# Windowed attention and feed-forward on one core: a handicap for VectorE in the planner's choice of engine, an own buffer for transposed blocks, no stores of A21, five late groups instead of six

## Chip, core and metric

The kernel runs on one NeuronCore of a Trainium2 chip. A core has TensorE (PE; its weight loads are shown as PEld), VectorE (DVE), ScalarE (ACT), GpSimd (POOL) and SyncE (SP), which here issues all DMAs from one queue. The metric is the device time of one execution in microseconds, the median of several; lower is better. All five engines run their own instruction streams in order and meet at semaphores.

## The reference

```
scores = q @ k^T / 8 + ALiBi bias, masked to 0 <= i - j < 128    # 8 batches, 8 heads, 576 tokens, 64 wide
attn   = softmax(scores);  x = attn @ v                           # -> x: 4608 tokens x 512
h      = x @ w_in                                                 # 512 x 2048
g      = h if h >= 1, 0 if h <= -1, else (h + 1)^2 / 4
out    = g @ w_out                                                # 2048 x 512
```

All of it is float32. The two weight matrices arrive as 64-bit numbers and are made float32 in the kernel.

## The kernel before, in words

**Work and stages.** The 4608 tokens are cut into nine chunks of 512. For each chunk there is attention (8 heads; head m is counted through all chunks, m = 0 to 71) and then a "sweep" of the feed-forward over eight groups g of two feature blocks. While chunk c is swept, the attention of chunk c + 1 is mixed in, so TensorE alternates between the two. Matrix products that need float32 are done in the rounded format FP32R with operands split into a rounded part and the rest (`rounded`, L362, and a subtraction), three products for one.

**First layer.** In chunk 0 each group multiplies four plain weight blocks A11, A12, A21, A22 with the token blocks B11 to B22. From chunk 1 on it uses a scheme of seven products (`PRODUCTS`, L30), whose weight operands are A11, A12, A22 and the four sums S1 to S4 of blocks (A21 enters only the sums). `build` (L506) makes a split operand in SBUF and stores it to a scratch buffer `d_<g>_<name>` in DRAM (shown as d_A and d_S); `fetch` (L519) brings it back in the later chunks (w_A, w_S). The ring of these operands has ten buffers, and `operands_upto` (L976) asks for them ten ahead.

**Early and late groups.** For the groups with g < 8 - LATE the sums are built during chunk 0 and fetched in chunk 1; there they pass the two buffers "o" that second-layer weights and outputs use too. For the last LATE groups (`late`, L981) the float32 weights are stored in chunk 0 (`spill`, d_w), loaded again in chunk 1 (`unspill`, L483) and the sums are built then, straight into the ring. LATE is 6 (L326).

**Attention.** Scores (L671 to L674), a masked copy (L680), a subtraction with the row minimum (L683) and the exponential (L687), the normalisation of z by the row sums (L698 on VectorE or four instructions L696 on ScalarE), a transposition of z, a split into lu0 and lu1 with masks on GpSimd (L705 on), and the product with v (L820), whose result is added into xn. Up to head 27 the transposition is TensorE's (p, L760); from head 28 (`TURN`) `turn_blocks` (L719) does it with VectorE's block transposition (L729) and two DMAs through DRAM (d_turn), in one buffer named turned.

**Second layer and activation.** `nonlinear` (L890): m = ReLU(h + 1) (L894 on VectorE or L895 on ScalarE), m squared (L897, ScalarE), h from it (L899), and the split into gh and gl. `layer2` multiplies gh and gl with the second-layer weights wo (L915 to L917, bank acc).

**What sets the order.** Every step is given to a planner (`Plan`) with its possible engines, each with a cost in microseconds, in the order of preference: `rounded` prefers ScalarE, the ReLU on SBUF prefers VectorE, the normalisation prefers VectorE. `forward` (L168) walks through time: whenever an engine e comes free it takes the ready step with the earliest due time. If e is not the step's first choice it asks first whether that choice would be done sooner (L222 to L226, the lines that the change touches):

```
queue = max(0.0, free[first] - t) + sum(...)          # what waits on the first choice
if queue + n.alts[first][0] < busy + 0.1:
    held_back = True
    continue
```

Twelve rounds with corrected due times are planned, the one that ends first is kept, and the program is written in its order: each engine runs its rows as they stand, whatever happens on the chip. So a change in one rule plans all engines anew.

**Shared buffers.** 17 buffers "w" (`NW`, L418) hold raw weights, the second-layer weights, the reloaded weights of the late groups (w32) and, once all of these have a place, the buffer turned (L724 to L726).

Of the kernel before, what the change touches and what calls it, by code (L numbers as in the profile page):

```python
# [9 lines left out]
F32 = mybir.dt.float32  # L10
# [19 lines left out]
PRODUCTS = (("A11", "B11"), ("A12", "B21"), ("S2", "T2"), ("S3", "T3"), ("S1", "T1"), ("S4", "B22"), ("A22", "T4"))  # L30
# [26 lines left out]
class Plan:  # L57


    CROSS, SAME, BACKLOG, STRETCH, SWAP, ROUNDS = 0.09, 0.04, 4.0, 2.0, 8.0, 12  # L60

    def __init__(self):
        self.nodes, self.slots, self.turn, self.common = [], {}, {}, {}
# [104 lines left out]
    def forward(self, engines, bandwidth):  # L168
        free = {e: 0.0 for e in engines}
# [11 lines left out]
        def room(n, t):  # L181
            b = n.need
            if b is None:
                return True
            free = sum(x <= t + 1e-9 for x, _ in slots[b.tag])
            return free > 0 and b.fits(free)

        def wake(e, t):
            nonlocal tick
            tick += 1  # L190
            heapq.heappush(events, (max(t, free[e]), tick, e))

        def enter(n):
            for e in n.alts:
                r = 0.0
                for d in n.deps:
                    r = max(r, d.end + (self.SAME if d.eng == e else self.CROSS))
                avail[e].append((n, r))
                wake(e, r)
# [6 lines left out]
        while events:  # L206
            t, _, e = heapq.heappop(events)
            if free[e] > t + 1e-9 or not avail[e]:
                continue
            if e == "SP" and pipe > t + self.BACKLOG:  # L210
                wake(e, pipe - self.BACKLOG)
                continue
            cands = [(n.late, n.index, n, r) for n, r in avail[e] if r <= t + 1e-9 and room(n, t)]
            if not cands:
                continue
            cands.sort(key=lambda x: x[:2])
            pick, held_back = None, False
            for late, _, n, r in cands:
                busy = n.alts[e][0]
                first = next(iter(n.alts))  # L220
                if first != e:
                    queue = max(0.0, free[first] - t) + sum(m.alts[first][0] for m, q in avail[first]  # L222
                                                            if m is not n and q <= t + 0.2 and m.late < n.late)
                    if queue + n.alts[first][0] < busy + 0.1:
                        held_back = True
                        continue  # L226
                worse = [(m, q) for m, q in avail[e] if q > t + 1e-9 and q < t + busy - 0.05 and m.late < late - 0.2
                         and m.late + slip < t + busy]
                if e in ("PE", "SP") or not worse:
                    pick = n  # L230
                    break
                soon = min(q for _, q in worse)
                if soon - t > 0.5 * busy:
                    pick = n
                    break
            if pick is None:
                soon = [q for _, q in avail[e] if q > t + 1e-9]
                wake(e, min(soon + [t + 0.2] if held_back else soon))
                continue
            if e == "DVE" and pick.alts[e][3] and lock["POOL"] > t + 0.15:  # L240
                for late, _, n, r in cands:
                    if not n.alts[e][3] and late < pick.late + self.SWAP and next(iter(n.alts)) == e:
                        pick = n
                        break
            n = pick
            busy, lat, _, port = n.alts[e]
            if port and e in lock:
                other = "POOL" if e == "DVE" else "DVE"
                held = max(0.0, lock[other] - t)
                busy, lat = busy + held, lat + held  # L250
                lock[e] = t + busy
            n.eng, n.start = e, t
            if e == "SP":
                pipe = max(pipe, t + lat) + port / bandwidth
                n.end = pipe + 0.2
            else:
                n.end = t + lat
            if n.need is not None:
                at = min((x for x in slots[n.need.tag] if x[0] <= t + 1e-9))
                slots[n.need.tag].remove(at)  # L260
                n.need.slot = at[1]
            for b in n.uses:
                if b.tag:
                    b.left, b.last = b.left - 1, max(b.last, n.end)
                    if not b.left:
                        slots[b.tag].append((b.last + self.CROSS, b.slot))
                        for x in engines:
                            wake(x, b.last + self.CROSS)
                    elif n.need is b:
                        for x in engines:  # L270
                            wake(x, t)
            free[e] = t + busy
            if e == "PE":
                slip = max(0.0, t - n.nominal)
            order.append(n)
            done += 1
            for x in n.alts:
                avail[x] = [a for a in avail[x] if a[0] is not n]
            wake(e, free[e])
            for s in n.next:  # L280
                waits[s] -= 1
                if waits[s] == 0:
                    enter(s)
# [13 lines left out]
def windowed_attention_then_ffn(  # L297
# [9 lines left out]
    nc = tc.nc  # L307
# [4 lines left out]
    P = 128  # L312
# [10 lines left out]
    NEG = -1.0e30  # L323
    LIGHT = 8
    FIRST = 1
    LATE = 6  # L326
    LO = D + 2
    TURN = 28
    assert set(SIZES) == {4}
# [1 line left out]
    plan = Plan()  # L331
    pools = {}
# [6 lines left out]
    def buf(pool, tag, n, shape, dtype, name):  # L339
        return plan.buf(pools[pool], tag, n, shape, dtype, name)  # L340
# [6 lines left out]
    def dve(n, f, port=False):  # L347
        return {"DVE": (n * 0.00104 + 0.068, n * 0.00104 + 0.155, f, port)}
# [13 lines left out]
    def rounded(n, out, src):  # L362

        alts = act(n, lambda: S.copy(out(), src()))  # L364
        alts.update(dve_fast(n, lambda: V.tensor_copy(out(), src())))
        return alts
# [7 lines left out]
    def dma(nbytes, f):  # L374
        return {"SP": (0.4, 2.8, f, nbytes)}
# [38 lines left out]
    w_of, wo_of, raw, fo, raws, kept = {}, {}, {}, {}, [], []  # L414
# [3 lines left out]
    NW = 2 * NFC + 1 - NFC  # L418
# [56 lines left out]
    scratch, sums_w, spilled, unspilled = {}, {}, {}, []  # L475
# [30 lines left out]
    def build(g, name):  # L506
        b, key, f = operand(g, name)
        if name in PLAIN or g >= NG - LATE:
            t = buf("ring", "r", 10, [P, 2, 2, P], F32R, f"b_{g}_{name}")
        else:  # L510
            t = buf("fp", "o", 2, [P, 2, 2, P], F32R, f"b_{g}_{name}")
        plan.op(rounded(2 * P, lambda: t.t[:, 0], f), [(b, key)], [(t, 0)])
        plan.op(dve(2 * P, lambda: V.tensor_tensor(t.t[:, 1], f(), t.t[:, 0].bitcast(F32), ALU.subtract), True),
                [(b, key), (t, 0)], [(t, 1)])
        d = scratch[g, name] = plan.buf(dr, f"d_{g}_{name}", 1, [P, 4 * P], F32, f"d_{g}_{name}")
        plan.op(dma(P * 2048, lambda: DMA.dma_start(d.t, t.t.bitcast(F32).rearrange("p s c f -> p (s c f)"))), [t], [d])
        return t
# [199 lines left out]
    turned = []  # L717

    def turn_blocks(m, z):  # L719


        if not turned:
            turned.append(plan.shared(pools["wp"], "w", NW, [P, 2, 4 * P], F32, "turned", lambda free: (
                all(x.slot is not None for _, x in kept) and all(x.slot is not None for x in unspilled))))  # L724
        t = turned[0]
        d = plan.buf(dr, "d_turn", 2, [P, 4 * P], F32, f"d_turn_{m}")  # L726

        def block():
            V.transpose(t.t[:, 0].rearrange("p (b i j) -> p b i j", b=4, i=4), z.t.rearrange("p i (s b) -> p b i s", b=4))  # L729

        plan.op(dve(4 * P, block, True), [z], [(t, 0)])
        plan.op(dma(P * 2048, lambda: DMA.dma_start(d.t, t.t[:, 0])), [(t, 0)], [d])
        plan.op(dma(P * 2048, lambda: DMA.dma_start(
            t.t[:, 1].rearrange("p (a e) -> p a e", a=4), d.t.rearrange("(a s) (b e) -> (s b) a e", a=4, b=4))), [d], [(t, 1)])
        return (t, 1), lambda: t.t[:, 1].rearrange("p (a i j) -> p i a j", a=4, i=4)
# [240 lines left out]
    def operands_upto(n):  # L976
        while asked[0] < min(n, len(todo_w)):
            c, g, x = todo_w[asked[0]]
            if c == 0 and x == "A11":
                weights_upto(4 * g + 2)  # L980
            late = g >= NG - LATE  # L981
            if late and c == 1 and x == "A11":
# [103 lines left out]
    for c in range(NCHUNK):  # L1086
        steps = sweep_steps(c)
        n = len(steps)
# [46 lines left out]
```

## Time and profile before

| | |
|---|---|
| median of 3 runs | 964.62 us (964.22 to 964.88) |
| profiled execution | 964.71 us, of which 963.0 us from the first to the last instruction (the span) |
| busy: PE / PEld / DVE / ACT / POOL | 951.1 / 863.4 / 869.9 / 661.4 / 218.5 us |
| moved by DMA | 227.40 MB, mean 236 GB/s |

How to read it: the profile is one execution. Every instruction belongs to a source line (L12 is line 12 of the kernel), an operation and tiles (out<-in, buffer numbers left out). Busy time of TensorE includes pipelining, so a busy TensorE can still be held up for a few tenths; its empty time is the part that can be read directly. "Idle" is followed by what ended it. The chain of waits is followed back from the last instruction. Times in the windows count from the start of the span.

### The profile page before, as it was taken

To read this page: it belongs to the slowest core of one execution; us is meant where nothing else is said; L and a number is where in the kernel's file an instruction comes from. 1 tells how busy PE (TensorE), PEld (TensorE's weight loads), DVE (VectorE), ACT (ScalarE), POOL (GpSimd) and SP (SyncE) were. 2 spreads that over 40 slices of the span, in tenths; PEclk is the share of its full clock that TensorE was granted. 3 is DMA by queue.
4 is the path that set the end of the run, shared out by engine and by line. 5 is a ranking of instruction groups with operands and counts; after the bars stand their busy time and mean duration, and the time that the engine had idled before them with its cause. 6 is when DMAs were issued, how large, how long until landed. Compare 5 with 4: busy or idle time off the path is not lost.

```text
span 963.0 us, 19573 instructions
## 1 busy us (share of the span) xinstructions
PE 951.1 (99%) x6320; PEld 863.4 (90%) x6320; DVE 869.9 (90%) x2183; ACT 661.4 (69%) x1657; POOL 218.5 (23%) x274
## 2 busy tenths in 40 slices
PE   8999999999999999999999999999999999999998
PEld 7889998999889998999899989899899999989987
DVE  6999999999999999999999999999999999984453
ACT  7998777877887677665876577667766777553322
POOL 2311111222331222322232212312232222210000
PEclk9999999999999999999999999999999999999999
DMA  9678886676867876887788869787888778766651
GB/s 345 235 244 276 300 269 204 229 220 222 246 204 255 253 243 211 284 259 245 223 278 254 255 212 279 244 255 223 257 276 251 218 233 272 225 174 201 174 152 44
DMA packets 133237, 227.40 MB, mean 236 GB/s; under 512 B 13712, under 2 KB 36240, under 8 KB 133136
## 3 DMA queue, kind: packets, MB, share of 16 engines
q1 hardware_dynamic: 133136, 226.15, 74.7%
q8 instruction: 51, 0.84, 0.3%
q14 instruction: 50, 0.41, 0.1%
HBM read 185.20 MB, written 40.89 MB: 235 GB/s over the span
## 4 chain that ended last, share of the span: by engine, by line
PE 83%; DVE 7%; ACT 6%; DMA 3%; issue 1%; POOL 0%; SPq 0%; ACTq 0%; DVEq 0%; POOLq 0%
PE hA L883 17%; PE hB L883 13%; PE acc L916 12%; PE acc L915 12%; PE acc L917 12%; PE x L820 6%; PE h L883 3%; PE s L673 2%; PE s L674 2%; ACT z L687 2%; PE s L671 1%; ACT raw L451 1%; DMA raw<-in_moe_w_out_dram 1%; PE p L760 1%; ACT raw L461 1%
## 5 line engine op out<-in xcount | busy, mean ns | idle before, releaser
L915 PE MATMUL acc<-wo,gh 128*128 128x512 f32 x576 | 228.0, 396 | 0.1
L916 PE MATMUL acc<-wo,gh 128*128 128x512 f32 x576 | 227.3, 395 | 0.0
L917 PE MATMUL acc<-wo,gl 128*128 128x512 f32 x576 | 225.7, 392 | 0.2
L708 POOL TENSOR_SCALAR_AFFINE_SELECT lu<-lu 128x512 fp32r<-128x512 f32 x112 | 100.6, 898 | 516.5 <-ACT lu L364 179.6
L1025 ACT COPY s<-hA 128x256 f32<-128x256 f32 x192 | 70.8, 369 | 98.7 <-PE hA L883 93.5
L687 ACT ACTIVATE z<-z,nmax 128x128 f32<-128x128 f32 x288 | 113.3, 395 | 26.9 <-DVE nmax L683 25.6
L917 PEld LDWEIGHTS acc<-wo,gl 128*128 128x128 f32 x576 | 108.2, 188 | 25.6 <-DVE gl L903 1.4
L915 PEld LDWEIGHTS acc<-wo,gh 128*128 128x128 f32 x576 | 108.9, 189 | 9.8 <-DVE o L923 0.3
L916 PEld LDWEIGHTS acc<-wo,gh 128*128 128x128 f32 x576 | 109.1, 189 | 8.8
L897 ACT ACTIVATE m<-m 128x512 f32<-128x512 f32 x144 | 90.6, 630 | 28.2 <-DVE m L894 26.3
L899 DVE SCALAR_TENSOR_TENSOR h<-h,m 128x512 f32<-128x512 f32 x128 | 95.0, 743 | 12.3 <-ACT m L897 11.7
L883 PEld LDWEIGHTS hA<-x_T,w_S 128*128 128x128 f32 x696 | 95.4, 190 | 8.7 <-ACT s L1025 3.1
L883 PE MATMUL hA<-x_T,w_S 128*128 128x256 f32 x696 | 102.2, 283 | 1.0 <-ACT s L1025 1.0
L1020 DVE TENSOR_TENSOR h<-hB,s 128x256 f32<-128x256 f32 x192 | 79.7, 415 | 24.8 <-PE hB L883 20.6
L903 DVE TENSOR_TENSOR gl<-h,gh 128x512 fp32r<-128x512 f32 x128 | 91.2, 713 | 1.9 <-ACT gh L364 0.7
L711 POOL TENSOR_SCALAR_AFFINE_SELECT lu<-lu 128x512 fp32r<-128x512 f32 x112 | 92.9, 851 | 0.0
L683 DVE CUSTOM_DVE_ANT_0 z<-s,rel 128x128 f32<-128x128 f32 x288 | 70.8, 282 | 0.5
L680 DVE COPY_PREDICATED s<-older,s 128x256 f32<-128x256 uint32 x144 | 59.8, 420 | 9.4 <-PE s L671 5.1
L364 ACT CAST gh<-h 128x512 fp32r<-128x512 f32 x75 | 46.5, 620 | 24.9 <-DVE h L899 24.0
L820 PE MATMUL x<-lu,vs 128*128 128x256 f32 (+3 forms) x560 | 62.8, 259 | 0.0
L820 PEld LDWEIGHTS x<-lu,vs 128*128 128x128 f32 (+1 forms) x560 | 57.4, 163 | 3.9 <-issue 0.2
L673 PE MATMUL s<-kk,ql 128*128 128x256 f32 x224 | 57.7, 281 | 1.0 <-DVE ql L598 0.7
(129 smaller groups left out, 2049.2 us busy)
## 6 DMA issues: line engine op xcount, KB each, us to landing
w_S<-d_S SPq DMA_DIRECT2D x232, 256.0 KB, 3.4
w_A<-d_A SPq DMA_DIRECT2D x192, 256.0 KB, 3.7
kr<-in_k_dram SPq DMA_DIRECT2D x112, 160.0 KB, 3.6
d_turn<-turned SPq DMA_DIRECT2D x44, 256.0 KB, 3.5
turned<-d_turn SPq DMA_DIRECT2D x44, 256.0 KB, 3.7
vn<-in_v_dram SPq DMA_DIRECT2D x33, 320.0 KB, 3.7
out_dram<-o SPq DMA_DIRECT2D x36, 256.0 KB, 4.1
qr<-in_q_dram SPq DMA_DIRECT2D x33, 256.0 KB, 4.2
```

Of the source, the lines that this page charges most:

```text
L687: plan.op({"ACT": (0.385, 0.48, lambda i=i: S.activation(z.t[:, i], z.t[:, i], AF.Exp, bias=nmax.t[:, i:i + 1], scale=-1.0, accum_out=sm.t ...
L708: G.affine_select(out=lu[s].t[:, 0:2 * nb:2], in_=a.bitcast(F32), pattern=[[0, nb], [-1, P]], base=0, channel_multiplier=1, compare_op=ALU ...
L711: G.affine_select(out=a, in_=a.bitcast(F32), pattern=[[0, nb], [1, P]], base=0, channel_multiplier=-1, compare_op=ALU.is_ge, fill=0.0)
L820: T.matmul(px[:rows, q0 * P:q1 * P], sv, mv.rearrange("p a w -> p (a w)"), start=(w == 0), stop=(w == len(todo) - 1), skip_group_check=True)
L883: T.matmul(o.t[:, at:at + 2 * P], w.t[:, a, kb], x.t[:, b, kb], start=start and n == 0, stop=stop and n == len(todo) - 1, skip_group_check ...
L897: plan.op(act_fn(n, lambda: S.activation(m.t, m.t, AF.Square, scale=0.5)), [m], [m])
L899: plan.op(dve(n, lambda: V.scalar_tensor_tensor(f.t, h.t, 1.0, m.t, ALU.max, ALU.min), not psum), src + [m], dst)
L903: plan.op(dve(n, lambda: V.tensor_tensor(gl.t, f.t, gh.t.bitcast(F32), ALU.subtract), True), dst + [gh], [gl])
L915: T.matmul(a.t, gh.t[:, ts], w.t[:, 0], start=first, stop=False)
L916: T.matmul(a.t, gh.t[:, ts], w.t[:, 1], start=False, stop=False)
L917: T.matmul(a.t, gl.t[:, ts], w.t[:, 0], start=False, stop=last)
L1020: plan.op(dve(2 * P, lambda: V.tensor_tensor(f.t[:, key * 2 * P:(key + 1) * 2 * P], b.t[:, :2 * P], s.t, ALU.add)), [b, s], [(f, key)])
```

## The change

- `forward` adds SPARE = 0.4 us to the time that VectorE is thought to need when VectorE is the first choice of a step and another engine asks for it. So ScalarE may take a step which VectorE would have done up to 0.4 us sooner.
- LATE is 5: group 2's sums are built in chunk 0. Its weights are no longer spilled and reloaded, and its four sums are fetched in chunk 1.
- `build` returns without a store for operands that are in no product of the later chunks, which is A21: eight stores fewer.
- turned has a buffer of its own instead of one of the 17.
- The scratch that is reserved for dynamic DMAs is set to 1024.

```
-    CROSS, SAME, BACKLOG, STRETCH, SWAP, ROUNDS = 0.09, 0.04, 4.0, 2.0, 8.0, 12
+    CROSS, SAME, BACKLOG, STRETCH, SWAP, ROUNDS, SPARE = 0.09, 0.04, 4.0, 2.0, 8.0, 12, 0.4
...
-                    if queue + n.alts[first][0] < busy + 0.1:
+                    if queue + n.alts[first][0] + (self.SPARE if first == "DVE" else 0.0) < busy + 0.1:
...
-    LATE = 6
+    LATE = 5
...
+        if all(name != w for w, _ in PRODUCTS):
+            return t
         d = scratch[g, name] = plan.buf(dr, f"d_{g}_{name}", 1, [P, 4 * P], F32, f"d_{g}_{name}")
...
-            turned.append(plan.shared(pools["wp"], "w", NW, [P, 2, 4 * P], F32, "turned", lambda free: (
-                all(x.slot is not None for _, x in kept) and all(x.slot is not None for x in unspilled))))
+            turned.append(buf("ap", "turned", 1, [P, 2, 4 * P], F32, "turned"))
...
-    nc = bacc.Bacc("TRN2", target_bir_lowering=False, num_devices=1)
+    nc = bacc.Bacc("TRN2", target_bir_lowering=False, num_devices=1, dynamic_dma_scratch_size=1024)
```

Below, rows of the written order. Names carry head or group numbers and a running number; lines behind L513 are one or two higher in the changed kernel (L828 is L829 there).

ScalarE, at the end of chunk 0's attention, before (raw: weights being scaled; xn_0<-x_7: values of head 7; x_0_B22: a rounded token block):

```order
L451 ACTIVATE raw_8_445<-raw_8_445 128x512
L461 ACTIVATE raw_8_445<-raw_8_445 128x512
L451 ACTIVATE raw_9_468<-raw_9_468 128x512
L687 ACTIVATE z_9_632,sum_9_646<-z_9_632,nmax_9_633 128x128
L828 COPY xn_0_322<-x_6_619 64x512
L687 ACTIVATE z_9_632,sum_9_646<-z_9_632,nmax_9_633 128x128
L461 ACTIVATE raw_9_468<-raw_9_468 128x512
L451 ACTIVATE raw_6_407<-raw_6_407 128x512
L828 COPY xn_0_322<-x_7_648 64x512
L461 ACTIVATE raw_6_407<-raw_6_407 128x512
L364 CAST x_0_B22_688<-xn_0_322 128x512
```

The same place on ScalarE in the changed kernel:

```order
L829 COPY xn_0_322<-x_6_595 64x512
L461 ACTIVATE raw_3_325<-raw_3_325 128x512
L451 ACTIVATE raw_8_446<-raw_8_446 128x512
L774 COPY lu_8_648<-p_8_623 128x512
L461 ACTIVATE raw_8_446<-raw_8_446 128x512
L451 ACTIVATE raw_6_405<-raw_6_405 128x512
L689 ACTIVATE z_9_656,sum_9_668<-z_9_656,nmax_9_657 128x128 x2
L461 ACTIVATE raw_6_405<-raw_6_405 128x512
L364 CAST x_0_B21_685<-xn_0_322 128x512
```

and on VectorE, which now has the copy of head 7's values:

```order
L855 TENSOR_TENSOR x_0_B12_468<-xn_0_322,x_0_B12_468 128x512
L830 COPY xn_0_322<-x_7_640 64x512
L513 TENSOR_TENSOR b_0_A12_529<-w_0_413,b_0_A12_529 128x256
L682 COPY_PREDICATED s_9_2_665<-older_100,s_9_2_665 128x2x128
L365 CAST x_0_B22_690<-xn_0_322 128x512
```

The scalings of raw_9 moved behind this place, the copy of head 7's values from ScalarE to VectorE, the copy of p_8 from VectorE to ScalarE, and the two rounded token blocks changed engines.

TensorE at the start of chunk 2's sweep, before (hA and hB: banks of the first layer; acc_1: second layer of chunk 1):

```order
L883 MATMUL hA_2_0_3795<-x_2_B11_3582,w_2_0_A11_3500 128x256 x6
L883 MATMUL hA_2_0_3795<-x_2_T2_3781,w_2_0_S2_3605 128x256 x6
L883 MATMUL hB_2_0_3828<-x_2_B21_3707,w_2_0_A12_3552 128x256 x6
L915 MATMUL acc_1_0_2551<-wo_6_1_1923,gh_1_14_3803 128x512
L916 MATMUL acc_1_0_2551<-wo_6_1_1923,gh_1_14_3803 128x512
L917 MATMUL acc_1_0_2551<-wo_6_1_1923,gl_1_14_3826 128x512
L820 MATMUL x_24_3853<-lu0_24_3750,vs_12_3681 128x256
```

and in the changed kernel, first the rows from the first product on, then the rows up to the T2 product:

```order
L884 MATMUL hA_2_0_3797<-x_2_B11_3593,w_2_0_A11_3507 128x256 x6
L884 MATMUL hB_2_0_3812<-x_2_B21_3704,w_2_0_A12_3554 128x256 x6
L916 MATMUL acc_1_0_2567<-wo_6_1_1937,gh_1_14_3754 128x512
L917 MATMUL acc_1_0_2567<-wo_6_1_1937,gh_1_14_3754 128x512
L918 MATMUL acc_1_0_2567<-wo_6_1_1937,gl_1_14_3773 128x512
L916 MATMUL acc_1_1_2577<-wo_6_1_1937,gh_1_14_3754 128x512
L917 MATMUL acc_1_1_2577<-wo_6_1_1937,gh_1_14_3754 128x512
L918 MATMUL acc_1_1_2577<-wo_6_1_1937,gl_1_14_3773 128x512
```

```order
L821 MATMUL x_24_3842<-lu0_24_3752,vs_12_3685 128x128
L821 MATMUL x_24_3842<-lu1_24_3763,vs_12_3685 66x128
L821 MATMUL x_24_3842<-lu1_24_3763,vs_12_3685 66x256
L821 MATMUL x_24_3842<-lu0_24_3752,vs_12_3685 128x256 x2
L821 MATMUL x_24_3842<-lu1_24_3763,vs_12_3685 66x256
L884 MATMUL hA_2_0_3797<-x_2_T2_3756,w_2_0_S2_3612 128x256 x6
```

The product with x_2_T2, which writes the same bank hA as the first one, moved from the second place to behind the B21 product, six layer-2 matmuls and head 24's values.

VectorE in chunk 0 of the changed kernel, beside the layer-2 steps of group 1 (w_2: float32 weights of group 2; b_2_S: its sums' split operands):

```order
L501 TENSOR_TENSOR S3_2_1176<-w_2_966 128x256
L472 TENSOR_TENSOR wo_1_1_1169<-fo_1_1_1128,wo_1_1_1169 128x512
L501 TENSOR_TENSOR S2_2_1189<-S1_2_1113,w_2_966 128x256
L464 ISA w_3_1173<-raw_12_522,w_3_1173 128x1024
L693 TENSOR_SCALAR rc_12_1200<-sum_12_1115 128x4
L900 SCALAR_TENSOR_TENSOR g_0_2_1202<-h0_0_2_1037,m_0_2_1137 128x512
L513 TENSOR_TENSOR b_2_S3_1196<-S3_2_1176,b_2_S3_1196 128x256
```

In the kernel before, these sums stand among chunk 1's rows, made from the reloaded w32_2:

```order
L501 TENSOR_TENSOR S2_2_2504<-S1_2_2212,w32_2_2147 128x256
L630 TENSOR_TENSOR vs_9_2473<-vn_9_2114,vs_9_2473 128x10x64
L365 CAST b_2_S2_2517<-S2_2_2504 128x256
L903 TENSOR_TENSOR gl_1_8_2523<-h1_1_0_2359,gh_1_8_2502 128x512
L785 TENSOR_TENSOR lu1_18_2534<-p_18_2497,lu0_18_2515 128x4x128
```

Eight VectorE steps of group 2, four roundings and four stores moved from chunk 1 to chunk 0.

## The prediction

> **What bounds the kernel now.** I read the page first, then the busy time by stretch, TensorE's waits, the chain of waits around the stretches where TensorE stood empty, and the groups by shape.
>
> ```profile
> span 963.0 us, 19573 instructions
> PE 951.1 (99%) x6320; PEld 863.4 (90%) x6320; DVE 869.9 (90%) x2183; ACT 661.4 (69%) x1657; POOL 218.5 (23%) x274
> ```
>
> TensorE is busy for 951.1 of 963.0 us, so 11.9 us are empty. The windows (start and end; width; busy time and instructions of PE, PEld, DVE, ACT, POOL; clock; DMA share; GB/s) say where they lie:
>
> ```profile
> 0.00:8.00 8.00, 6.34 (x28) 6.14 (x29) 3.22 (x13) 2.93 (x4) 2.17 (x18) 1.00 0.75 242
> 8.00:16.00 8.00, 7.04 (x39) 5.47 (x38) 7.22 (x43) 6.36 (x27) 1.35 (x3) 1.00 1.03 393
> 32.00:40.00 8.00, 6.43 (x45) 5.33 (x44) 7.88 (x34) 7.95 (x28) 2.97 (x4) 1.00 0.59 218
> 48.00:56.00 8.00, 6.71 (x47) 6.19 (x48) 7.44 (x21) 7.98 (x21) 1.60 (x2) 1.00 0.66 227
> 56.00:64.00 8.00, 7.75 (x57) 7.20 (x57) 7.90 (x22) 7.93 (x20) 1.34 (x2) 1.00 0.76 216
> 72.00:144.00 72.00, 72.00 (x481) 66.06 (x480) 69.54 (x176) 56.35 (x127) 9.67 (x10) 1.00 0.84 280
> 144.00:260.00 116.00, 115.65 (x789) 105.24 (x788) 112.72 (x301) 88.91 (x224) 26.59 (x32) 1.00 0.72 225
> 260.00:276.00 16.00, 14.85 (x103) 13.41 (x102) 15.88 (x37) 12.71 (x30) 6.11 (x7) 1.00 0.59 192
> 276.00:840.00 564.00, 563.19 (x3787) 512.77 (x3787) 541.46 (x1318) 396.53 (x1012) 152.66 (x178) 1.00 0.80 248
> 864.00:888.00 24.00, 24.00 (x150) 21.56 (x149) 12.90 (x26) 9.74 (x20) 0.00 (x0) 1.00 0.61 187
> 840.00:963.00 123.00, 119.32 (x730) 106.27 (x728) 68.00 (x126) 42.60 (x87) 5.66 (x8) 1.00 0.50 150
> ```
>
> The granted clock is 1.00 in each. Empty time: 2.6 us up to 16 us; 1.57 + 1.29 + 0.25 = 3.1 in 32:40, 48:56 and 56:64, where ScalarE is busy for over 7.9 of 8 us; none in 72:144; 0.35 in 144:260; 1.15 in 260:276; 0.81 in the next 564 us; 3.68 after 840, the last copy and store. VectorE is over 96% busy from 72 to 840 us, yet TensorE is as full there as in 864:888, where VectorE has half the load. A group of six first-layer matmuls takes 0.72 us on the chain at 193 us and 0.71 us at 872 us:
>
> ```profile
> 193.54 0.72 PE hA L883 x6
> 872.49 0.71 PE hA L883 x6
> ```
>
> So the bound is TensorE, 951 us of work that the change leaves as it is. What can be won is the empty time outside the first 16 us and the tail: 3.1 + 0.35 + 1.15 + 0.81 and the few tenths in 16:32 and 40:48, 5.6 us in all.
>
> **The change, part by part.** *The handicap.* Counted over the two orders, VectorE has 28 ReLU steps fewer (L894) and nine normalisations fewer (L698); ScalarE has 28 more (L895) and nine times four more (L696). In the other direction VectorE takes 17 rounding casts more, which the planner gives it in the room that comes free.
>
> ```profile
> L894 DVE TENSOR_SCALAR m<-h 128x512 f32<-128x512 f32 x86 | 38.1, 442 | 14.2 <-ACT h L1031 13.7
> L895 ACT ACTIVATE m<-h,one 128x512 f32<-128x512 f32 x58 | 41.5, 716 | 10.9 <-PE h L883 4.6 <-DVE h L1020 3.3 <-DVE rc L692 2.1
> L698 DVE TENSOR_TENSOR z<-z,rc 128x512 f32<-128x512 f32 x57 | 39.0, 685 | 0.3
> L696 ACT ACTIVATE z<-z,rc 128x128 f32<-128x128 f32 x60 | 19.2, 395 | 2.5 <-DVE rc L692 2.5
> L365 DVE CAST lu<-turned 128x512 fp32r<-128x512 f32 x19 | 8.0, 421 | 1.3 <-DMA turned<-d_turn 1.3
> ```
>
> VectorE gives off 28 × 0.442 + 9 × 0.685 = 18.5 us and takes back about 17 × 0.42 = 7.1: net 11 us of 870 (ten more casts and copies that leave it add some 5). ScalarE takes 28 × 0.716 + 36 × 0.32 (19.2 / 60) = 31.6 us less the casts. A ReLU costs 0.27 us more where it now runs, and the work of both engines grows. None of it is on TensorE; it tells only where TensorE waits.
>
> The Trainium skill (Perfetto Trace Analysis, § Optimizing Scalar/DVE Operations) says that where VectorE has a fast mode it is the quicker engine, and that handing work to ScalarE may pay when VectorE is saturated. The rows agree on the first (0.442 against 0.716 us); in the first 64 us it is ScalarE that is full, and there the same sentence speaks against the change.
>
> TensorE's waits (us in total, times, longest) name what some gaps are worth:
>
> ```profile
> PE hA L883 <- ACT s L1025: 1.0, 3, 0.5
> PE s L673 <- DVE ql L598: 0.7, 1, 0.7
> ```
>
> *260 to 276 us* holds one of the three waits for the copy L1025 and the one for L598. The chain there is VectorE without a break:
>
> ```profile
> 262.41 0.49 DVE h L899
> ...
> 264.11 0.95 DVE x_T L854
> ...
> 271.66 0.73 DVE kl L615
> 272.39 0.60 DVE xn L834
> ...
> 273.02 0.70 DVE ql L598
> ```
>
> Before, the T2 product of chunk 2's first group follows the A11 product on the same bank hA at once, so it waits for the copy of that bank and for x_T2. After, the B21 product, six layer-2 matmuls and the ten matmuls of head 24's values stand between. Ahead of the T2 product VectorE has five instructions fewer: five ReLUs and two normalisations left, and a few casts came. I take the whole 1.15 us away. Bounds: 0 (another wait takes the place) and 1.15.
>
> *The start.* Up to the second product of the first group (h0 with x_0_B21) the new order has 9 + 9 weight scalings on ScalarE where there were 12 + 11, no normalisation instead of four, and the copy of head 7's values runs on VectorE instead of standing behind two scalings in ScalarE's queue. The chain at that place was:
>
> ```profile
> 45.26 0.57 ACT raw L461
> 45.84 0.56 ACT raw L451
> 46.40 0.02 issue
> 46.42 0.58 ACT xn L828
> ...
> 47.62 0.60 ACT x_B L364
> ```
>
> Five scalings of 0.57 and four scalings of z at 0.32 are 4.1 us less ahead; five other steps come in. But ScalarE gets the scalings back later, and three more ReLUs follow by the 13th head's transpose. Of the 3.1 us I take 0.6 (half of the 1.29 in 48:56); bounds −1.3 (all of 48:56) and +2.0 (rival B).
>
> *Elsewhere* (0.35 + 0.81 us, some of them at chunk borders that the order leaves as they were): in the written order, the reads by TensorE that stand within 1 us of TensorE's work behind the step that wrote their tile (TensorE's steps priced by their spacing in the trace) fall from 139 to 112. I take 0.4 away; bounds −1.1 and +1.0.
>
> *LATE 5.* Group 2's four sums, their rounding, their low parts and their four stores come from chunk 1 to chunk 0, by the layer-2 steps of groups 0 and 1 that they now stand beside, into 72:144.
>
> ```profile
> L501 DVE TENSOR_TENSOR S<-w 128x256 f32<-128x256 f32 x16 | 8.4, 529 | 0.0
> L513 DVE TENSOR_TENSOR b_S<-S,b_S 128x256 fp32r<-128x256 f32 x32 | 14.0, 446 | 0.3 <-ACT b_S L364 0.2
> d_A<-b_A SPq DMA_DIRECT2D x32, 256.0 KB, 3.8
> w_S<-d_S SPq DMA_DIRECT2D x232, 256.0 KB, 3.4
> d_S<-b_S SPq DMA_DIRECT2D x32, 256.0 KB, 3.2
> ```
>
> On VectorE 4 × 0.53 + 4 × 0.45 = 3.9 us, in a stretch with 72 − 69.5 = 2.5 us of room on it. The operands are for chunk 1, far behind; a step of chunk 0 queued behind them on VectorE is late by at most 3.9 − 2.5 = 1.4 us, if the room lies elsewhere. The four blocks now also pass the two buffers o, which chunk 0's second-layer weights need; a weight behind one of them waits for its store, 3.2 us, but TensorE stood nowhere in 72:144. I take 0, since two ReLUs leave VectorE in chunk 0 too; upper bound 3.2. The four new fetches in chunk 1 stand ten operands ahead of their use and land in 3.4 us; TensorE's waits name no transfer. Cost 0.
>
> *A21 not stored; one spill and one unspill less:* eight stores of d_A, two of d_w and one load of w leave SP's queue; by the first product of chunk 1 it has 129 transfers ahead, not 135. For the same reason 0, bounds −0.35 (all of 144:260) and 0. *Own buffer for turned blocks:* the first and last starts (behind min/median/max ns) of the transposes and of the loads that had to come before them are
>
> ```profile
> L729 DVE STREAM_TRANSPOSE turned<-z x44: 1077/1108/1123, 301.3 to 834.7; 128x512 f32<-128x512 f32 x44
> L488 SPq DMA_DIRECT2D w<-d_w x6: 319/320/707, 153.7 to 241.1; - x6
> ```
>
> so the old slot was free 60 us ahead of its first use: 0. The smaller DMA scratch only makes room.
>
> **Sum.** −1.15 − 0.6 − 0.4 = −2.15 us on the profiled execution's 964.71 (span 963.0 and 1.7 around it): 962.5 us. That execution lies 0.1 above the median of 964.62.
>
> **Rivals.**
> *A. The gaps move.* The order is planned anew everywhere, each gap is below 1.3 us, and new hand-overs can be as tight; the regular gaps at chunk borders speak for it. Then nothing changes beyond 1.9 us: 964.2.
> *B. ScalarE becomes the start's bound (slower).* In 32:64 it has under 0.1 us of room in 8. By the 13th head's transposes the new order gives it three ReLUs and two scalings more, less four normalisations: 3 × 0.716 + 2 × 0.57 − 4 × 0.32 = 2.0 (four casts and copies net come too, for which VectorE has less); with no gain elsewhere 964.71 + 2.0 = 966.7. It decides where ScalarE's load up to the first layer-2 matmuls passes VectorE's. For it: the chain rows of 45 to 48 us are ScalarE's. Against it: up to the second product ScalarE has less ahead than before.
> *C. VectorE is the true bound.* Then its 11 us come off: 953.5. 90% on VectorE is as much as PEld's 90%; against it stands 864:888 above, TensorE no faster with VectorE half idle. The Trainium skill (Perfetto Trace Analysis, § Identifying the Most-Contended Engine) counts weight loading rather than matmul busy time for TensorE, and by that both engines are level, which is this rival; the trace's equal 0.71 and 0.72 us say no.
> *D. The change doesn't do what it says:* for the own buffer and the stores that is the case, as far as time goes (0 above); for the handicap the counts exclude it.
>
> **Chances and range.** Forecast (the gaps close by more than they open, gain over 1.9) 0.47; C 0.03; A (within 1.9 either way) 0.33; B 0.17. About 0.2%, 1.9 us, is what a measurement of this kernel can tell from no change, so faster 0.50, same 0.33, slower 0.17. My terms are the middle of each gap, so the forecast stands at the near end of its own range of 960.0 to 962.7; the far end has 4.7 of the 5.6 us gone. To hold 8 in 10 the range takes in all of A and the mild part of B and leaves out C: 960.0 to 966.0.
>
> ```profile
> L897 ACT ACTIVATE m<-m 128x512 f32<-128x512 f32 x144 | 90.6, 630 | 28.2 <-DVE m L894 26.3
> ```
>
> **What would show it.** Right: 260:276 with TensorE full; 48:56 emptier by no more than 0.7; VectorE's busy time 10 to 18 us lower, ScalarE's 25 to 33 higher; ScalarE's 26.3 us of waiting for VectorE's ReLU (the row above) shorter; SP's issues d_A 24 instead of 32. Wrong: empty time in 32:64 over 4 us with ScalarE at its end (B); new waits of TensorE over 0.5 us after 276 us (A); matmul groups under 0.71 us or a gain over 6 us (C).

## The result and the profile after

The changed kernel takes 971.15 us (median of 5 runs, 970.23 to 971.46), the kernel before 964.22 beside it (5 runs, 963.43 to 964.88). The ratio is 1.0071, interval 1.0057 to 1.0085: slower by 6.9 us, where 2.1 us less were forecast. The profiled execution took 971.46 us. The head of its page:

```profile
span 969.7 us, 19537 instructions
PE 952.5 (98%) x6320; PEld 862.4 (89%) x6320; DVE 854.2 (88%) x2153; ACT 684.1 (71%) x1714; POOL 211.7 (22%) x274
```

VectorE does 15.7 us less, ScalarE 22.7 more, and TensorE's work is nearly the same; its empty time has grown from 11.9 to 17.2 us. The windows of the changed kernel, columns as before (the prediction has no row for 24:72 and the last two):

```profile
32.00:40.00 8.00, 5.67 (x43) 4.91 (x42) 7.42 (x29) 7.95 (x27) 3.01 (x4) 1.00 0.48 187
48.00:56.00 8.00, 7.77 (x59) 7.25 (x59) 7.67 (x27) 8.00 (x23) 1.60 (x2) 1.00 0.59 207
24.00:72.00 48.00, 44.71 (x322) 40.95 (x321) 45.00 (x153) 47.51 (x127) 11.28 (x15) 1.00 0.67 241
144.00:260.00 116.00, 113.95 (x780) 104.25 (x780) 109.25 (x293) 89.61 (x227) 26.71 (x34) 1.00 0.69 221
260.00:276.00 16.00, 15.92 (x108) 14.26 (x107) 15.94 (x38) 11.96 (x30) 6.83 (x8) 1.00 0.57 184
276.00:840.00 564.00, 559.18 (x3741) 506.70 (x3740) 529.11 (x1292) 407.21 (x1041) 146.25 (x177) 1.00 0.80 245
500.00:528.00 28.00, 27.39 (x185) 24.68 (x185) 25.79 (x63) 16.36 (x44) 8.71 (x10) 1.00 0.77 243
590.00:636.00 46.00, 44.30 (x293) 39.74 (x291) 41.36 (x104) 30.06 (x81) 13.15 (x16) 1.00 0.82 257
```

The gain at 260 to 276 us came (1.15 us empty before, 0.08 now). The start gave nothing (48 - 44.71 = 3.29 us empty in 24:72; 3.27 before). The loss is where the forecast saw a full TensorE: 4.82 us empty in 276:840 (0.81 before) and 2.05 in 144:260 (0.35). TensorE's waits name new writers (total, times, longest):

```profile
PE hA L884 <- ACT s L1026: 1.9, 6, 0.5
PE hB L884 <- DVE h L1021: 1.5, 4, 0.4
PE acc L916 <- ACT o L923: 1.4, 2, 1.1
```

**First place: group 3 of chunks 3 to 6.** The first two rows stand for a place that comes back once a chunk. In chunk 4 TensorE waits there twice, for the T2 product (hA) and the T3 product (hB):

```profile
512.42 0.98 PE L884 MATMUL hA<-x_T,w_S 128*128 128x256 f32 x6 [0.24 <-ACT s L1026]
513.78 0.98 PE L884 MATMUL hB<-x_T,w_S 128*128 128x256 f32 x6 [0.38 <-DVE h L1021]
```

What the two writers stood behind is in the timelines of their engines. ScalarE, changed kernel:

```profile
508.71 0.63 ACT L898 ACTIVATE m<-m 128x512 f32<-128x512 f32 x1
509.98 0.63 ACT L898 ACTIVATE m<-m 128x512 f32<-128x512 f32 x1 [0.64 <-DVE m L895]
510.64 0.58 ACT L834 COPY xn<-x 64x512 f32<-64x512 f32 x1
511.24 0.73 ACT L631 CAST vs<-vn 128x640 fp32r<-128x640 f32 x1
512.00 0.37 ACT L1026 COPY s<-hA 128x256 f32<-128x256 f32 x1
```

VectorE, changed kernel:

```profile
509.52 0.43 DVE L895 TENSOR_SCALAR m<-h 128x512 f32<-128x512 f32 x1
...
510.86 0.68 DVE L700 TENSOR_TENSOR z<-z,rc 128x512 f32<-128x512 f32 x1
511.57 0.68 DVE L835 TENSOR_TENSOR xn<-x,xn 64x512 f32<-64x512 f32 x1
512.29 1.13 DVE L730 STREAM_TRANSPOSE turned<-z 128x512 f32<-128x512 f32 x1
513.31 0.41 DVE L1021 TENSOR_TENSOR h<-hB,s 128x256 f32<-128x256 f32 x1
```

The same place in the kernel before, VectorE:

```profile
509.08 0.42 DVE L1020 TENSOR_TENSOR h<-hB,s 128x256 f32<-128x256 f32 x1
509.52 0.68 DVE L834 TENSOR_TENSOR xn<-x,xn 64x512 f32<-64x512 f32 x1
510.24 1.11 DVE L729 STREAM_TRANSPOSE turned<-z 128x512 f32<-128x512 f32 x1
```

and ScalarE, where the copy of bank hA (L1025) comes ahead of the second square (L897):

```profile
507.55 0.73 ACT L629 CAST vs<-vn 128x640 fp32r<-128x640 f32 x1
508.30 0.37 ACT L1025 COPY s<-hA 128x256 f32<-128x256 f32 x1
...
509.09 0.63 ACT L897 ACTIVATE m<-m 128x512 f32<-128x512 f32 x1
```

Two things changed places. The group's two ReLUs: before, VectorE took the first block's and ScalarE the second's; now the other way round, so ScalarE stands 0.64 us with its square waiting for VectorE's ReLU, and the copy that frees bank hA is queued behind that and behind two more steps (before, it stood behind the same two steps, but ahead of the square). And the sum that frees bank hB (L1021) now stands behind the value sum and the 1.1 us transpose, where it stood ahead of them. The matmuls after a wait also look longer (0.98 us for six where 0.87 is usual), so the empty time shows only part of the loss: the starts of TensorE's rows, set side by side in the two traces, fall back by 1.22, 1.15, 0.64 and 1.14 us at the four places, 4.15 us in all (the expectations below take 0.94 to 1.10 us for each). It is only 0.64 in chunk 5 because the kernel before waits there too: one of its three waits for the copy of bank hA, 0.26 us at 610.21 us, stands in this very group.

**Second place: the output stores at a chunk's end.** SP's queue in the changed kernel, chunk 4:

```profile
588.50 0.42 SPq L927 DMA_DIRECT2D out_dram<-o  x1
589.02 1.12 SPq L556 DMA_DIRECT2D kr<-in_k_dram  x2
590.23 0.54 SPq L524 DMA_DIRECT2D w_S<-d_S  x1
590.86 0.38 SPq L927 DMA_DIRECT2D out_dram<-o  x1
```

Two loads of k stand between the stores of the first and second output block; before, they stood behind the fourth store:

```profile
585.04 0.42 SPq L926 DMA_DIRECT2D out_dram<-o  x1
586.35 0.34 SPq L926 DMA_DIRECT2D out_dram<-o  x1
...
592.28 0.34 SPq L926 DMA_DIRECT2D out_dram<-o  x1
...
593.48 1.18 SPq L554 DMA_DIRECT2D kr<-in_k_dram  x2
```

ScalarE's copy of the fourth bank needs the second block's buffer o, and TensorE the bank. The chain of waits in the changed kernel (start, length, what):

```profile
590.86 5.95 DMA out_dram<-o
...
596.88 0.09 ACT o L923
```

**Third: 132 to 172 us**, 2.46 us empty where 0.35 were. There ScalarE stands still for a raw weight fetch:

```profile
139.46 0.68 ACT L451 ACTIVATE raw<-raw 128x512 f32<-128x512 f32 x1 [4.13 <-DMA raw<-in_moe_w_in_dram]
```

**Theories.** H: these places of single steps, in the order that the handicap led to, are the loss. L: the end of chunk 0 with the late sums is. W: the work moved to the slower engine costs by its amount. N: any new plan of the same work brings new small waits.

### The profile page after: what moved, and what is told of

It reads as the page before. It is cut to its first block, busy times and chain, and to the rows that moved or that the text cites. A ratio compares the mean times of both kernels' runs of the same rounds, so it can differ in the third digit from the quotient of the medians.

```text
span 969.7 us, 19537 instructions
## 1 busy us (share of the span) xinstructions
PE 952.5 (98%) x6320; PEld 862.4 (89%) x6320; DVE 854.2 (88%) x2153; ACT 684.1 (71%) x1714; POOL 211.7 (22%) x274
## 4 chain that ended last, share of the span: by engine, by line
PE 73%; DVE 12%; ACT 7%; DMA 5%; issue 2%; SPq 1%; POOL 0%; DVEq 0%; ACTq 0%; POOLq 0%
PE hA L884 15%; PE hB L884 11%; PE acc L917 11%; PE acc L916 11%; PE acc L918 11%; PE x L821 5%; PE h L884 2%; PE s L675 2%; PE s L676 2%; ACT z L689 2%; PE s L673 1%; DMA out_dram<-o 1%; DMA turned<-d_turn 1%; DMA w_S<-d_S 1%; DVE h L900 1%
## 5 line engine op out<-in xcount | busy, mean ns | idle before, releaser
L710 POOL TENSOR_SCALAR_AFFINE_SELECT lu<-lu 128x512 fp32r<-128x512 f32 x112 | 95.4, 852 | 528.0 <-DVE lu L365 171.0
L1021 DVE TENSOR_TENSOR h<-hB,s 128x256 f32<-128x256 f32 x192 | 79.7, 415 | 39.9 <-PE hB L884 33.2
L884 PE MATMUL hA<-x_T,w_S 128*128 128x256 f32 x708 | 104.2, 283 | 1.9 <-ACT s L1026 1.9
L898 ACT ACTIVATE m<-m 128x512 f32<-128x512 f32 x144 | 90.6, 630 | 20.6 <-DVE m L895 19.3
L900 DVE SCALAR_TENSOR_TENSOR h<-h,m 128x512 f32<-128x512 f32 x128 | 90.2, 705 | 16.8 <-ACT m L898 16.5
L713 POOL TENSOR_SCALAR_AFFINE_SELECT lu<-lu 128x512 fp32r<-128x512 f32 x112 | 91.0, 834 | 0.0
L896 ACT ACTIVATE m<-h,one 128x512 f32<-128x512 f32 x86 | 61.6, 717 | 10.4 <-DVE h L1021 5.3
```

The costliest lines, as they stand in the source:

```text
L710: G.affine_select(out=lu[s].t[:, 0:2 * nb:2], in_=a.bitcast(F32), pattern=[[0, nb], [-1, P]], base=0, channel_multiplier=1, compare_op=ALU ...
L713: G.affine_select(out=a, in_=a.bitcast(F32), pattern=[[0, nb], [1, P]], base=0, channel_multiplier=-1, compare_op=ALU.is_ge, fill=0.0)
L884: T.matmul(o.t[:, at:at + 2 * P], w.t[:, a, kb], x.t[:, b, kb], start=start and n == 0, stop=stop and n == len(todo) - 1, skip_group_check ...
L898: plan.op(act_fn(n, lambda: S.activation(m.t, m.t, AF.Square, scale=0.5)), [m], [m])
L900: plan.op(dve(n, lambda: V.scalar_tensor_tensor(f.t, h.t, 1.0, m.t, ALU.max, ALU.min), not psum), src + [m], dst)
L1021: plan.op(dve(2 * P, lambda: V.tensor_tensor(f.t[:, key * 2 * P:(key + 1) * 2 * P], b.t[:, :2 * P], s.t, ALU.add)), [b, s], [(f, key)])
```

## The experiments

All comparisons are with runs of the kernel before on the same chip. Line numbers of profiles differ where lines were added.

**e1, the handicap alone**, on the kernel before.

```
-                    if queue + n.alts[first][0] < busy + 0.1:
+                    if queue + n.alts[first][0] + (self.SPARE if first == "DVE" else 0.0) < busy + 0.1:
```

> The kernel before with the handicap of 0.4 us alone (LATE 6, A21 stored, turned blocks in the shared slots). Theory H, the handicap's new order carries the loss: the written order has the same two places at group 3 of chunks 3 to 6 as the changed kernel (the bank sum of the A12 product behind the 1.1 us transpose on VectorE, the bank copy on ScalarE behind a square that waits for VectorE's ReLU), worth 0.94 to 1.10 us a chunk in the profile after, 3.9 us in all, so 967.5 to 970. Theory L, the end of chunk 0 carries it (five groups' sums late, stores left out): 964 to 966, as these parts are not in it. Theory N, any new plan moves the small waits about: anything from 962 to 970, and no relation to group 3.

969.72 us against 965.06, ratio 1.0046 (1.0034 to 1.0058): 4.4 us of the 6.9, in the range of H and in the wide one of N. Both places are in its trace (1.19, 0.61, 1.73 and 0.76 us empty in 396:420, 500:528, 590:636 and 690:728, where the kernel before has 0, 0, 0.57 and 0), and 256:324 has none, so the gain there is the handicap's too.

**e2, all but the handicap.** The whole change, with

```
-    CROSS, ..., ROUNDS, SPARE = 0.09, ..., 12, 0.4
+    CROSS, ..., ROUNDS = 0.09, ..., 12
...
-                    if queue + n.alts[first][0] + (self.SPARE if first == "DVE" else 0.0) < busy + 0.1:
+                    if queue + n.alts[first][0] < busy + 0.1:
```

> The changed kernel with the handicap set to nothing, the other three parts left. Theory H: the waits at group 3 are gone, since the bank sum stands ahead of the transpose again, and the time is 963.5 to 965.5. Theory L: the 1.7 us lost between 140 and 160 us stay, 965.5 to 967.5. Theory N: anything from 962 to 970.

966.54 against 965.06, ratio 1.0015 (1.0006 to 1.0023): the time lies in the range of L and 1.0 us above that of H. In those four windows it has 0.12, 0, 0.36 and 0 us empty, so H's places are gone, and its 1.5 us are lost elsewhere. Windows of e2 (the profiled execution, 968.94 us, is the slowest of its twelve):

```profile
72.00:144.00 72.00, 72.00 (x479) 66.09 (x478) 67.73 (x173) 57.47 (x132) 8.71 (x9) 1.00 0.80 263
256.00:324.00 68.00, 65.75 (x437) 58.54 (x436) 63.89 (x160) 51.28 (x125) 18.71 (x20) 1.00 0.69 219
```

The late sums are made in 72:144, and TensorE is full there; 132:172, where L expected the loss of 1.7 us to stay, has 0.56 empty (0.35 before). What grew is 256:324, to 2.25 us from 1.15, and 24:72, to 4.07 from 3.27, and neither is where the change put work. So L's number came, but not in L's place.

**e3, own buffer and smaller scratch alone**, on the kernel before.

```
-            turned.append(plan.shared(pools["wp"], "w", NW, ...))
+            turned.append(buf("ap", "turned", 1, [P, 2, 4 * P], F32, "turned"))
```

> The kernel before with the own buffer for the turned blocks and the smaller DMA scratch alone: the order of every engine is that of the kernel before, row by row. All theories: 964.2, within 0.7. If the changed kernel's first 12 us, which came 1.06 us earlier than before, are owed to where the buffers lie, this one shows them too: 963.2.

964.95 against 965.06, ratio 0.9999 (0.9990 to 1.0007): nothing, as forecast. Its rows behind 12 us come 0.6 us earlier than in the trace of before, and in e6, with the same order there, 1.1: the first microseconds are an execution's own.

**e4, two steps moved ahead at group 3 of the changed kernel.**

```
     order = self.schedule(engines, bandwidth)
+    for step, ahead_of in self.pulled():
+        order.remove(step)
+        order.insert(order.index(ahead_of), step)
...
+    for c in range(3, 7):     # copy of bank hA ahead of L834, sum of bank hB ahead of L835
+        plan.pull += [(("s", c, 3, 0), ("xs", 8 * c + 11)), (("add", c, 3, 1), ("xn", 8 * c + 11))]
```

> The changed kernel with two steps moved ahead in each of chunks 3 to 6, everything else in its place: at group 3 the sum of the A12 bank goes on VectorE ahead of head 11's value sum and the transpose, and the copy of the A11 bank on ScalarE ahead of head 11's value copy and the 0.73 us cast of v. Theory H, the places of these two steps are what TensorE waits for: the waits of 0.40 to 0.56 and 0.54 us go in each of the four chunks, 3.9 us less, 967.2 (3.0 to 3.9 less). A rival, the two engines are full there and only pass the delay on to the next step: under 1 us less, 970.2 to 971.2, with new waits in the same groups.

968.08 against 965.06, ratio 1.0033 (1.0021 to 1.0044). The changed kernel itself has 1.0071 and, on another chip (e8), 1.0076: eight instructions moved take back 0.38 to 0.43%, 3.7 to 4.1 us, at or just above the upper end of what H expected. The waits of e4:

```profile
PE acc L925 <- ACT o L932: 2.9, 4, 1.2
...
PE hA L893 <- ACT s L1035: 0.6, 2, 0.3
```

The wait for the sum (hB) is gone from the list, that for the copy is 0.6 instead of 1.9. TensorE's 6320 matmuls stand in the same order in both traces: at the four places those of e4 gain 1.29, 1.14, 1.14 and 1.15 us on the changed kernel's first profile, 4.7 us in all. H's first place is shown, and it is worth 4 to 5 us. The traces differ elsewhere too, and what they gain and lose there nearly cancels: 132:172 has 2.0 us less empty, the stretches 324:396 and 420:500 have 1.0 us more, and the waits for the output's banks have grown from 1.4 to 2.9.

**e5, the loads of k behind the stores too.**

```
+    for c in range(2, 6):
+        plan.push += [(("kr", 4 * c + 11, 1, r), ("out", c, 3)) for r in (64, 0)]
```

> The changed kernel with the two steps at group 3 moved ahead (as in the run before) and, for chunks 2 to 5, the two loads of kr1 that the new order puts between the output stores o_0 and o_1 on SP's queue (chunk 2: between o_1 and o_2) put back behind the fourth store, where the kernel before has them. Theory H with a second place: the first layer-2 matmul of the next chunk's fourth block waits for the copy of that bank, which waits for a buffer o, whose store is issued behind these loads; in the profile of the run with group 3 mended these waits are 0.50, 0.70, 1.36 and 1.02 us, 3.6 us in all. They go: 2.5 to 3.6 us less than that run, 0 to 1 us above the kernel before. Rival, the store is late for the load on the DMA engines and not for its place: less than 1 us of the 3.6 goes, 2.5 to 4 us above the kernel before.

967.33 against 965.04, ratio 1.0022 (1.0007 to 1.0038). The times show 1.0 us where H expected 2.5 at the least and its rival less than 1, and the intervals of e4 and e5 overlap. In the trace the waits are gone: no row for acc is left in TensorE's list, and 500:528 and 690:728 are full:

```profile
500.00:528.00 28.00, 28.00 (x191) 25.67 (x191) 26.25 (x65) 16.05 (x43) 8.95 (x11) 1.00 0.81 257
690.00:728.00 38.00, 38.00 (x258) 34.45 (x257) 35.58 (x88) 24.93 (x66) 10.73 (x13) 1.00 0.86 278
```

So the second place is real, but little of it is won. Set beside those of e4, TensorE's rows gain 0.2, 0.8, 1.5 and 1.1 us at the four stores (391, 493, 595 and 696 us) and lose 1.0, 0.9 and 0.3 about 10 us behind the first, third and fourth, where TensorE now waits for the copy of bank hA (1.5 us in the list for 0.6 in e4). Part of the delay is passed on, and this execution also has 0.85 us more empty in 132:172.

**e6, the reverse test: the transpose ahead of the sum in the kernel before.**

```
+    for c in range(3, 7):
+        plan.pull += [(("xn", 8 * c + 11), ("add", c, 3, 1)), (("turn", 8 * c + 13), ("add", c, 3, 1))]
```

> The kernel before, nothing else changed, with the other order of the one place at group 3: in each of chunks 3 to 6 head 11's value sum and the 1.1 us transpose stand ahead of the sum of the A12 bank on VectorE (before: the sum first). The sum ends 1.8 us later than at 509.5 us, 1.0 us behind the start that the T3 product has at 510.27 us. Theory H: 1.0 us in each of four chunks, 3 to 4.1 us slower. Rival, the place is only a sign of other load: within 1 us of the kernel before.

970.00 against 965.04, ratio 1.0051 (1.0033 to 1.0069): 5.0 us slower from four sums that stand two rows later. TensorE's waits in e6:

```profile
PE hB L894 <- DVE h L1031: 5.6, 6, 1.6
```

The place alone makes the loss, without a handicap and with no work moved between engines. Its size is above the expected 3 to 4.1, though the interval (3.2 to 6.7 us) reaches into that range; TensorE's rows fall back by 1.80, 1.18, 1.24 and 1.20 us at the four places.

**e7, a handicap of 0.3 us.** The whole change, with

```
-    CROSS, ..., ROUNDS, SPARE = 0.09, ..., 12, 0.4
+    CROSS, ..., ROUNDS, SPARE = 0.09, ..., 12, 0.3
```

> The changed kernel with a handicap of 0.3 us for 0.4. Counted in the written order, ScalarE takes 75 of the 144 first ReLU steps (58 before, 86 at 0.4) and 20 normalisations (15 and 24), so well over half of the moved work is moved; but at group 3 the A12 bank's sum stands ahead of the transpose in all four chunks, and the kr1 loads stand behind the stores. Theory H, the places decide and not the amount: 0 to 2 us above the kernel before. Rival W, the work moved to ScalarE costs the time by its amount: 17 of 28 ReLUs moved, so 17/28 of 6.9 us, about 4.2 us above the kernel before.

969.86 against 965.04, ratio 1.0046 (1.0029 to 1.0064): H's number was wrong, and W's 4.2 us came close. But not by W's mechanism spread over the span: 500:528 and 690:728 are full, and the greatest loss is at the start, in the windows of e7:

```profile
24.00:72.00 48.00, 43.19 (x306) 38.99 (x305) 42.40 (x148) 47.71 (x131) 10.99 (x16) 1.00 0.64 231
```

4.81 us are empty there (3.27 before) with ScalarE at 47.71 of 48 us; 324:396 has 1.24 (0.06 before) and 728:836 has 0.97 (0). Different places again, which made N the theory to test.

**e8, the changed kernel again**, beside e5 to e7.

> The changed kernel as it is, beside the others on one chip. 6 to 7 us above the kernel before, with waits at group 3 of chunks 3 to 6 (0.9 to 1.1 us a chunk) and at the fourth block's bank (1.8 us in all), as in its profile. The 2.4 us that were lost between 132 and 172 us, where a 512 KB weight fetch took 9.7 us to land, are not in the plan (the same order had them not in the run with group 3 mended): if they come back, they belong to the plan after all.

972.48 against 965.04, ratio 1.0076 (1.0058 to 1.0094), just above the 6 to 7 us expected, with 1.48, 0.61, 1.36 and 1.31 us empty in the four windows of e1 and 1.41 in 132:172. That last stretch has the same written order in four of these kernels, and its empty time goes with the landing of the two 512 KB weight fetches issued in 124:148:

| | e4 | e5 | e8 | changed, first profile |
|---|---|---|---|---|
| median from issue to landing, us | 7.0 | 7.8 | 7.9 | 9.7 |
| TensorE empty in 132:172, us | 0.45 | 1.30 | 1.41 | 2.46 |

As far as four executions show, the plan leaves no slack to that transfer, and its landing time decides what the stretch costs.

**e9 to e11, the kernel before planned anew without any part of the change.**

```
-    CROSS, SAME, ... = 0.09, 0.04, ...
+    CROSS, SAME, ... = 0.10, 0.04, ...   # e9;  e10: 0.09, 0.05;  e11: 0.08, 0.04
```

> The kernel before with one number of the planner changed, the cost of a hand-over between engines, 0.10 us for 0.09; no part of the change is in it. The written order is new (5580 of 6130 of TensorE's rows stand in common, 1710 of 2185 of VectorE's); 67 ReLU steps on ScalarE (58 before), 7 normalisations (15); neither of the two bad places at group 3 and at the stores. Theory N, a new plan of the same work brings new small waits whatever made it new: 1.5 to 5 us above the kernel before, as the run with all but the handicap (1.5) and the one with 0.3 (4.8). Theory W, the amount of work moved to ScalarE costs: ScalarE has 9 ReLUs more and 8 times four scalings fewer, so within 1 us of the kernel before.

> The kernel before with another number of the planner changed, the cost of a hand-over on one engine, 0.05 us for 0.04; no part of the change is in it. 61 ReLU steps and 12 normalisations on ScalarE, exactly the counts of the run with all but the handicap, and most rows in common with the kernel before (6055 of 6130 on TensorE). Theory N: 0.5 to 3 us above the kernel before, in places of its own. Theory W: within 1 us.

> The kernel before with the cost of a hand-over between engines at 0.08 us for 0.09; no part of the change is in it. 62 ReLU steps and 5 normalisations on ScalarE, 5604 of 6130 of TensorE's rows in common. Theory N: 1.5 to 5 us above the kernel before. Theory W: within 1 us, below it if anything, since ScalarE has 40 scalings fewer.

e9: 966.52 against 964.62, ratio 1.0023 (1.0013 to 1.0032). e10: 964.47, ratio 1.0000 (0.9991 to 1.0010). e11: 968.84, ratio 1.0042 (1.0028 to 1.0056). With nothing changed but a planner's constant, a plan costs 0 to 4.1 us. In all three ScalarE is busy for less time than before (656.9, 660.1 and 658.8 us against 661.4). N holds for two of three; e10, which keeps nearly all rows, misses its range by half a microsecond. W has nothing for it. These are three plans, and all are set against one; whether the plan of the kernel before is better than most is not on record, so the spread tells what leaving that plan costs, and nothing of a mean.

**e12, the kernel before with two steps moved by hand at 260 to 276 us.**

```
+    plan.pull += [(("prod", 2, 0, 1), ("prod", 2, 0, 2))]     # TensorE: B21 product ahead of T2
+    plan.pull += [(("ql", 13, 0), ("xn", 24))]                # VectorE: ql of head 26 ahead of L834
```

> The kernel before with two steps moved by hand at 260 to 276 us, where the changed kernel gained: on TensorE the A12 product (with B21) of chunk 2's first group ahead of the T2 product, and on VectorE the second half of head 26's q ahead of head 24's value sum. In the profile before, TensorE waits 0.62 us ahead of the T2 product and 0.84 us ahead of head 26's scores. Both theories of places: 0.6 to 1.4 us of the 1.15 us empty in 256:324 go, 963 to 964.5 where the kernel before has 964.2 to 965; the profile can tell it, the times hardly. Rival, the delay is passed on to the T1 and T3 products behind them: empty time in 256:324 stays at 1 us.

964.82 against 964.62, ratio 0.9999 (0.9990 to 1.0009). Its window and its waits:

```profile
256.00:324.00 68.00, 66.78 (x452) 60.80 (x451) 65.81 (x166) 50.87 (x125) 18.82 (x20) 1.00 0.78 235
```

```profile
PE hB L894 <- DVE h L1031: 0.8, 1, 0.8
```

1.22 us are still empty: the rival was right that the delay is passed on, though not to the products that it named. The B21 product, now ahead, waits 0.8 us for VectorE's sum, and head 26's scores wait 0.4 for the value sum that was put behind. Here VectorE is busy 65.81 of 68 us, and the chain of waits is VectorE's from 261.64 to 273.69 us. In the changed kernel the B21 product stands in the same place and waits for nothing, so that move on TensorE does not explain the gain by itself. At group 3 (e4) the same kind of move won all of it, where the steps put behind were presumably not waited for so soon; that was only argued, not tried. No version here is measurably faster than the kernel before.

## Why the prediction was wrong

Where TensorE was empty in each profile, us (width less TensorE's busy time):

| | before | changed | changed, e8 | e4 | e5 |
|---|---|---|---|---|---|
| up to 24 | 2.62 | 2.78 | 2.62 | 3.23 | 2.64 |
| 24:72 | 3.27 | 3.29 | 3.05 | 3.33 | 2.97 |
| 132:172 | 0.35 | 2.46 | 1.41 | 0.45 | 1.30 |
| 256:324 | 1.15 | 0.08 | 0.08 | 0.08 | 0.08 |
| 324:396 and 420:500 | 0.13 | 0.47 | 1.84 | 1.44 | 0.53 |
| 396:420, 500:528, 590:636, 690:728 | 0.57 | 4.04 | 4.76 | 2.06 | 1.22 |
| the rest, with the end | 3.79 | 4.04 | 3.77 | 3.91 | 3.87 |

- **260 to 276 us, -1.15:** right in its number. Measured -1.07, and e1 shows that it is the handicap's. Of the two reasons given, e12 tried a part of the first (TensorE's order) and the gap stayed; the second (five instructions fewer on VectorE) was not tried alone.
- **The start, -0.6:** wrong by its size. 48:56 did fill (0.23 us empty instead of 1.29), but 32:40 (2.33 instead of 1.57) and 40:48 (0.41 instead of 0.09) lost as much, and 24:72 is level. Rival B did not come at 0.4; at 0.3 it did (e7).
- **Elsewhere, -0.4 with bounds of -1.1 and +1.0:** this is the step that failed. It counted how many of TensorE's reads stand within 1 us behind their writer in TensorE's own order, and that count fell from 139 to 112. But at group 3 TensorE's order hardly changed; the writers moved back in their own engines' queues, behind a transpose and behind a square that waits for the other engine. The count cannot see that. Nor did the prediction place the other two of the three waits for the copy, one of which was at group 3 already. Measured: +5.7 us empty where -0.4 was forecast (+1.7 in 144:260, +4.0 in 276:840), and 3.7 to 4.1 us of time from group 3 alone (e4; in the kernel before, 5.0 from the place of the sum alone, e6).
- **LATE 5, stores of A21, own buffer, 0 each:** the own buffer is 0 by itself (e3). The other two came with a plan of their own that costs 1.5 us (e2), mostly in 256:324 and 24:72, not in the steps that were costed. The bound for the stores of -0.35 to 0 in 144:260 was too tight: 132:172 depends on the landing of a transfer (e8).
- **Rival A** named the mechanism, new hand-overs as tight as the old ones, and was priced at "within 1.9 us" with nothing to bear that out. Plans with no part of the change cost 0, 2.2 and 4.1 us more.
- **Rivals C and D** are out, and the engines' sums came nearly as forecast (VectorE -15.7 for 10 to 18; ScalarE +22.7 for 25 to 33). ScalarE's waiting for VectorE's ReLU fell as said, in the group's row after:

```profile
L898 ACT ACTIVATE m<-m 128x512 f32<-128x512 f32 x144 | 90.6, 630 | 20.6 <-DVE m L895 19.3
```

19.3 us for 26.3, while the time rose: a total over the span did not tell of the one wait per chunk that mattered.

A rule of the Trainium skill fits one half of this (Perfetto Trace Analysis, § Tensor Engine Instruction): it calls ScalarE's and VectorE's queues strict FIFO, and the copy at 512.00 us behind a square that waits 0.64 us agrees with it. Another (the same page, § Optimization Strategy) says that the same gap coming back on the engine that should be full can mean too few buffers. At group 3 no buffer was needed: e4 moved eight instructions, gave none, and the gap went. Whether another bank would have closed it too was not tried.

**What stays open:** what e5 still loses, 2.1 us (0.7 to 3.7). It lies within what a new plan costs without any part of the change, but its waits were not all taken apart. The second place's price in time is not settled either: the waits for the stores can go, and the time follows only in part.

## What to carry to other kernels

When a planner orders all engines, a changed rule is a new plan, and its price is the plan's, not the sum of the moved steps: plan the old work anew with a neutral constant first, and take that spread (here 0 to 4.1 us over three plans) as the least uncertainty of any forecast. Compare the two orders not by the bound engine's rows but by what stands ahead of each writer it waits for, in that writer's queue, above all in the groups that come back in every chunk, since half a microsecond there counts four times. A pass over the finished order that moves a few steps is a clean test: it changes nothing else in the written order.

## What the runs showed that was not expected

- Eight steps two rows earlier (e4) or four two rows later (e6), on engines that are busy 71 to 90% of the time, were worth 4 and 5 us of 965.
- The same kernel and order can find its 512 KB fetches landing after 7.0 to 9.7 us in one stretch, and where ScalarE's queue waits for them TensorE loses 0.4 to 2.5 us.
- The kernel before took 961.95 to 968.06 us over the runs beside the experiments, a wider spread than its first runs (964.22 to 964.88) let expect.
